# A fused SwiGLU feed-forward kernel: gate and up slices regrouped from 1, 2, 3, 3, 3 to 1, 1, 2, 4, 4 f chunks, two fillers ahead of the first projection dropped

## Chip, cores and metric

The kernel runs on one core of one Trainium2 chip. The metric is the device time of one execution in microseconds (us). A profiled execution also has a span, from the first to the last instruction, which is about 1.3 us shorter than its device time (162.8 against 164.1 for the profiled run of before).

## Reference

```python
B, S, D, F = 1, 2048, 640, 1536          # bf16
def reference(x, w_gate, w_up, w_down):
    g = silu(x @ w_gate)
    u = x @ w_up
    return (g * u) @ w_down
```

## The kernel before

F is cut into 12 chunks of 128 columns, S into four blocks of 512 rows. For each block and each f chunk, five matmuls make the gate projection `pg` and five the up projection `pu`; ScalarE and VectorE make `aT` from them; then `aT` is multiplied by the down weights. Weights stay resident after one load, in column slices of which each becomes usable only when all of it has landed. The first block is the special one: x comes in rows and is transposed by the tensor engine, and everything waits for first loads. The cut below is shortened, also between the lines that it shows.

```python
W_CHUNKS = [(0, 1), (1, 3), (3, 6), (6, 9), (9, 12)]   # f chunks per slice
N_WARM, N_GAP = 18, 2
...
load_x(nc.sync, 0, 1); load_x(nc.scalar, 2, 3)          # four chunks of 128 rows of x
load_x(nc.sync, 1, 2); load_x(nc.scalar, 3, 4)
for dst, src in ((wg_sb, wg_v), (wu_sb, wu_v)):         # slice 0 on both queues
    for eng, (k0, k1) in zip(queues, halves):
        eng.dma_start(out=dst[:, k0:k1, wslice(0, 1)], in_=src[:, k0:k1, wslice(0, 1)])
load_w(nc.sync, wg_sb, wg_v, *W_CHUNKS[1])              # slice 1: gate, then up
load_w(nc.sync, wu_sb, wu_v, *W_CHUNKS[1])
for a, b in W_CHUNKS[2:]:
    load_w(nc.sync, wg_sb, wg_v, a, b); load_w(nc.sync, wu_sb, wu_v, a, b)
nc.sync.dma_start(out=wd_sb[:], in_=wd_v)
... # cut
def warm(n):                                            # fillers: results unused
    for _ in range(n):
        nc.tensor.matmul(pw[:, 0:P], lhsT=ones[:], rhs=ones[:], start=True, stop=True)
... # cut; the head of the tensor engine, first block and first f chunk:
warm(N_WARM)
transpose_chunk(0, [(dve, "po_a", 0, KD)])
transpose_chunk(2, [(dve, "po_b", 0, KD)])
warm(N_GAP)
for c in (1, 3):
    transpose_chunk(c, [(act, "po_a", 0, 2), (dve, "po_b", 2, KD)])
warm(2)
proj_pair(pg, wg_sb, fc, sb, 0)                         # 5 matmuls, x chunks 0 and 2
proj_pair(pg, wg_sb, fc, sb, 1)                         # 5 matmuls, x chunks 1 and 3
proj(pu, wu_sb, fc, sb, 0, S_BLK)
```

## Time and profile before

| | before |
|---|---|
| time, first three runs | 163.87 us median (163.78 to 164.17) |
| span of the profiled run | 162.8 us |
| tensor engine busy | 98% |
| first projection starts | 5.30 us |
| second f chunk starts | 7.49 us |

A line of the timeline has the start in us, the duration in us, the engine, the line of the kernel, the operation, output and inputs, and how many were merged; brackets tell the idle time before it and what ended that. How fast the tensor engine ran is read from merged lines: ten 128-column matmuls at half rate start 107 ns apart and take about 1.27 us in all, at full rate 56 ns apart and 0.72 to 0.76 us; a gap between them makes a line longer. The tensor engine goes from half to full rate; this text calls that moment the release of the clock. The prediction shows the line of the second ten transposes (0.76 us, full rate). The first ten, from the tensor engine's timeline of the kernel before:

```profile
2.28 1.27 PE L189 MATMUL pt<-ident,x_sb 128*128 128x128 bf16 x10
3.35 0.42 PE L180 MATMUL pw<-ones 128*128 128x128 bf16 x2
```

1.27 us for ten is half rate, and so is 0.42 us for two. So in this one execution the clock was released between 3.35 and 4.23 us.

### The profile page before, as it was taken

Reading aid. Unit: us, or ns where it says so; the run is one execution under the profiler, and the core shown is the slowest. Engines: PE = TensorE matmul, PEld = TensorE weight load, DVE = VectorE, ACT = ScalarE, POOL = GpSimd, SP = SyncE. Lnnn points to the kernel's source line nnn. Section 1 sums busy time; section 2 is a strip of 40 time slices with the busy share of each in tenths; the row PEclk is TensorE's granted clock in tenths of the full one; section 3 lists DMA queues with packets and bytes.
Section 4 is the critical chain, followed back from the end, with each engine's and each line's share of the span. In section 5 each row is a group of like instructions: output and inputs, shape, how many; then the busy total and the mean of one; then the engine's idle time right before and its main releaser. Section 6 shows DMA issues by size and latency. Waiting matters only on the chain.

```text
span 162.8 us, 2081 instructions
## 1 busy us (share of the span) xinstructions
PE 159.7 (98%) x779; PEld 75.4 (46%) x779; DVE 111.8 (69%) x251; ACT 42.6 (26%) x73; POOL 0.6 (0%) x6
## 2 busy tenths in 40 slices
PE   8999999999999999999999999999999999999994
PEld 7644444444444444444444444444444444445442
DVE  2223333499559999979919999979964999993000
ACT  3322222212232222221222322221214222222121
POOL 1000000000000000000000000000000000000000
DMA  7999999993269993003110000000420000000312
GB/s 212 295 327 330 364 216 253 245 185 60 66 152 180 220 220 68 4 0 34 64 64 0 0 4 2 0 0 0 64 68 32 0 0 0 0 0 4 53 35 73
DMA packets 42585, 15.86 MB, mean 97 GB/s; under 512 B 33232, under 2 KB 42448, under 8 KB 42576
## 3 DMA queue, kind: packets, MB, share of 16 engines
q1 hardware_dynamic: 33664, 14.75, 37.2%
q10 hardware_dynamic: 8912, 0.98, 4.0%
q8 instruction: 6, 0.10, 0.3%
q14 instruction: 3, 0.02, 0.1%
HBM read 7.21 MB, written 2.62 MB: 60 GB/s over the span
## 4 chain that ended last, share of the span: by engine, by line
PE 95%; DMA 3%; SPq 0%; DVE 0%; issue 0%
PE pu L198 32%; PE pg L198 31%; PE po_a L281 25%; PE po_t L256 6%; DMA wg_sb<-in_w_gate_dram 3%; PE pg L213 1%; SPq L84 0%; PE po_b L298 0%; DVE ot_b L306 0%
## 5 line engine op out<-in xcount | busy, mean ns | idle before, releaser
L198 PE MATMUL pu<-xT,wu_sb 128*128 128x512 bf16 (+1 forms) x240 | 59.5, 379 | 0.0
L198 PE MATMUL pg<-xT,wg_sb 128*128 128x512 bf16 (+1 forms) x235 | 58.3, 379 | 0.0
L246 DVE TENSOR_TENSOR aT<-sg,pu 128x512 bf16<-128x512 f32 (+1 forms) x48 | 32.8, 683 | 32.0 <-PE pu L198 32.0
L245 ACT ACTIVATE sg<-pg 128x512 f32<-128x512 f32 (+1 forms) x48 | 28.6, 596 | 70.2 <-PE pg L198 65.7
L281 PE MATMUL po_a<-wd_sb,aT 128*128 128x512 bf16 x192 | 42.1, 379 | 0.0
L151 DVE SCALAR_TENSOR_TENSOR prod<-wgT,x_row 128x640 f32<-128x640 bf16 x48 | 39.4, 821 | 1.1
L151 DVE SCALAR_TENSOR_TENSOR prod<-wuT,x_row 128x640 f32<-128x640 bf16 x48 | 39.4, 821 | 1.0
L198 PEld LDWEIGHTS <-wu_sb 128*128 128x128 bf16 x240 | 23.5, 98 | 28.0
L198 PEld LDWEIGHTS <-wg_sb 128*128 128x128 bf16 x235 | 23.0, 98 | 27.6
L281 PEld LDWEIGHTS <-aT 128*128 128x128 bf16 x192 | 18.8, 98 | 22.5
L289 ACT CAST ot<-po_a 128x512 bf16<-128x512 f32 x16 | 9.4, 586 | 32.3 <-PE po_a L281 21.3
L256 PE MATMUL po_t<-aT,wd_sb 128*128 128x512 bf16 (+1 forms) x48 | 10.4, 366 | 0.0
L256 PEld LDWEIGHTS <-wd_sb 128*128 128x128 bf16 x48 | 4.7, 98 | 5.1
L306 DVE CAST ot_b<-po_b 128x128 bf16<-128x128 f32 x1 | 0.3, 291 | 9.9 <-PE po_b L298 9.9
L265 ACT CAST ot_t<-po_t 128x512 bf16<-128x512 f32 (+1 forms) x4 | 2.2, 560 | 11.6 <-PE po_t L256 11.6
L194 DVE COPY xT<-pt 128x640 bf16<-128x640 bf16 (+1 forms) x4 | 1.6, 425 | 3.4 <-PE pt L189 3.4
L151 DVE DVE_READ_ACCUMULATOR prod<-wuT,x_row 128x1 f32 x48 | 3.9, 82 | 0.0
L151 DVE DVE_READ_ACCUMULATOR prod<-wgT,x_row 128x1 f32 x48 | 3.9, 82 | 0.0
L267 DVE STREAM_TRANSPOSE ot_q<-ot_t 128x512 bf16<-128x512 bf16 (+1 forms) x4 | 2.7, 678 | 1.7 <-ACT ot_t L265 1.7
L180 PE MATMUL pw<-ones 128*128 128x128 bf16 x22 | 2.8, 304 | 0.4 <-DVE ones L104 0.4
L189 PE MATMUL pt<-ident,x_sb 128*128 128x128 bf16 x20 | 2.0, 268 | 0.5 <-DMA x_sb<-in_x_dram 0.5
L180 PEld LDWEIGHTS <-ones 128*128 128x128 bf16 x22 | 2.2, 143 | 0.4 <-DVE ones L104 0.4
(17 smaller groups left out, 9.0 us busy)
## 6 DMA issues: line engine op xcount, KB each, us to landing
out_dram<-ot SPq DMA_DIRECT2D x16, 128.0 KB, 1.7
wd_sb<-in_w_down_dram SPq DMA_DIRECT2D x1, 1920.0 KB, 12.6
wg_sb<-in_w_gate_dram SPq DMA_DIRECT2D x3, 480.0 KB, 7.1
wu_sb<-in_w_up_dram SPq DMA_DIRECT2D x3, 480.0 KB, 7.6
x_row<-in_x_dram SPq DMA_DIRECT2D x1, 640.0 KB, 4.8
out_dram<-ot_q ACTq DMA_DIRECT2D x12, 32.0 KB, 1.9
x_sb<-in_x_dram SPq DMA_DIRECT2D x2, 160.0 KB, 3.0
x_sb<-in_x_dram ACTq DMA_DIRECT2D x2, 160.0 KB, 3.2
```

Source lines behind the costliest of these rows:

```text
L151: nc.vector.scalar_tensor_tensor(out=prod[:], in0=wT[:, fc, :], scalar=1.0, in1=x_row[:, t, :], op0=ALU.mult, op1=ALU.mult, accum_out=acc[ ...
L180: nc.tensor.matmul(pw[:, 0:P], lhsT=ones[:], rhs=ones[:], start=True, stop=True)
L189: nc.tensor.transpose(out=pt[:, kd - k0, :], in_=x_sb[:, c, kd * P : (kd + 1) * P], identity=ident[:],)
L198: nc.tensor.matmul(ps[:, c0:c1], lhsT=w_sb[:, kd, fc * P : (fc + 1) * P], rhs=xT[:, kd, sb * S_BLK + c0 : sb * S_BLK + c1], start=(kd == 0 ...
L213: nc.tensor.matmul(pair(ps[:]), lhsT=w_sb[:, kd, fc * P : (fc + 1) * P], rhs=pair(xT[:, kd, sb * S_BLK : (sb + 1) * S_BLK]), start=(kd == ...
L245: nc.scalar.activation(sg[:, 0:n_s], pg[:, 0:n_s], ACT.Silu)
L246: nc.vector.tensor_tensor(out=aT[:, fc, s_sl], in0=sg[:, 0:n_s], in1=pu[:, 0:n_s], op=ALU.mult)
L256: nc.tensor.matmul(po_t[:], lhsT=wd_sb[:, kf, DA:D], rhs=aT[:, kf, sb * S_BLK : sb * S_BLK + n_t], start=(kf == 0), stop=(kf == KF - 1),)
L265: nc.scalar.copy(ot_t[:], po_t[:])
L267: nc.vector.transpose(out=ot_q[:], in_=ot_t[:])
L281: nc.tensor.matmul(po_a[:], lhsT=aT[:, kf, s0 : s0 + P], rhs=wd_sb[:, kf, 0:DA], start=(kf == 0), stop=(kf == KF - 1),)
L289: nc.scalar.copy(ot[:], po_a[:])
```

## The change

The intent is to have the second gate and up slices sooner (half the bytes), to make up for it with larger slices where there is slack, and to let the first projection start as soon as its slice is there.

```diff
-    W_CHUNKS = [(0, 1), (1, 3), (3, 6), (6, 9), (9, 12)]
+    W_CHUNKS = [(0, 1), (1, 2), (2, 4), (4, 8), (8, 12)]
@@ head of the tensor engine
                 for c in (1, 3):
                     transpose_chunk(c, [(act, "po_a", 0, 2), (dve, "po_b", 2, KD)])
-                warm(2)
                 proj_pair(pg, wg_sb, fc, sb, 0)
```

## The prediction

> **What bounds the kernel now.** I read the page first, then the waits of the tensor engine, then the timeline of the first 36 us, then the DMA issues and packet counts in short windows of the head. From the page, the header, the busy line and the chain of work that ended last:
>
> ```profile
> span 162.8 us, 2081 instructions
> ...
> PE 159.7 (98%) x779; PEld 75.4 (46%) x779; DVE 111.8 (69%) x251; ACT 42.6 (26%) x73; POOL 0.6 (0%) x6
> ...
> PE 95%; DMA 3%; SPq 0%; DVE 0%; issue 0%
> PE pu L198 32%; PE pg L198 31%; PE po_a L281 25%; PE po_t L256 6%; DMA wg_sb<-in_w_gate_dram 3%; PE pg L213 1%; SPq L84 0%; PE po_b L298 0%; DVE ot_b L306 0%
> ```
>
> The chain is tensor-engine work from end to end, except for one DMA: the load of the first gate slice, 3% of the span. Who made the tensor engine wait, over the whole span:
>
> ```profile
> PE pt L189 <- DMA x_sb<-in_x_dram: 0.5, 1, 0.5
> PE pw L180 <- DVE ones L104: 0.4, 1, 0.4
> PE pg L213 <- DMA wg_sb<-in_w_gate_dram: 0.2, 1, 0.2
> ```
>
> Three waits, 1.1 us in all, all in the first 5.3 us. There is no wait for a second or later weight slice, and none after the first projection started. So the kernel is a head of about 5.3 us followed by an unbroken stream of matmuls. A change to weight slices or fillers can gain only in the head, and can lose only if it opens a gap in the stream. The timeline of the head and of the first f chunks:
>
> ```profile
> 0.39 2.10 PE L180 MATMUL pw<-ones 128*128 128x128 bf16 x18 [0.39 <-DVE ones L104]
> ...
> 0.91 0.43 SPq L118 DMA_DIRECT2D wg_sb<-in_w_gate_dram  x1
> ...
> 2.18 0.37 SPq L81 DMA_DIRECT2D wg_sb<-in_w_gate_dram  x1
> ...
> 2.64 0.47 SPq L81 DMA_DIRECT2D wu_sb<-in_w_up_dram  x1
> ...
> 4.23 0.76 PE L189 MATMUL pt<-ident,x_sb 128*128 128x128 bf16 x10 [0.46 <-DMA x_sb<-in_x_dram]
> ...
> 4.83 0.28 PE L180 MATMUL pw<-ones 128*128 128x128 bf16 x2
> ...
> 5.30 1.27 PE L213 MATMUL pg<-xT,wg_sb 128*128 128x256 bf16 x10 [0.20 <-DMA wg_sb<-in_w_gate_dram]
> ...
> 7.27 0.96 PEld L198 LDWEIGHTS <-wg_sb 128*128 128x128 bf16 x5
> ...
> 8.35 0.96 PEld L198 LDWEIGHTS <-wu_sb 128*128 128x128 bf16 x5
> ```
>
> Two things are to be seen. First, the two fillers that the change drops start at 4.83 and are over at 5.11, and the first projection still waits 0.20 us after them, for the gate slice whose first half was issued at 0.91. Second, the second gate and up slices, issued at 2.18 and 2.64, are first read by the weight loads at 7.27 and 8.35. When they landed comes from the DMA issues of the window from 2.1 to 2.9 us (KB each, then us from issue to landing):
>
> ```profile
> wg_sb<-in_w_gate_dram SPq DMA_DIRECT2D x1, 320.0 KB, 4.6
> wu_sb<-in_w_up_dram SPq DMA_DIRECT2D x1, 320.0 KB, 5.3
> ```
>
> That is 2.18 + 4.6 = 6.8 and 2.64 + 5.3 = 7.9 us: 0.5 and 0.4 us ahead of need. These are the tightest deadlines among the later weight slices. The third slices, read the same way in the window from 4.1 to 4.8, landed at 4.20 + 5.2 = 9.4 and 4.61 + 6.3 = 10.9 against first uses at 11.59 and 12.67.
>
> **What the Trainium skill says.** "DMA: Bandwidth & Descriptors", section Specifications, gives 512 B as the smallest transfer for line rate. A one-chunk slice has rows of 128 bf16, 256 B, so the change puts two more loads below it. The trace agrees that packet size sets the rate. Packet counts in three windows, 4.3 to 5.0 us (about half 256 B), 5.0 to 7.0 (nearly all 512 B), and 8 to 14 (nearly all 768 B):
>
> ```profile
> DMA packets 468, 0.17 MB, mean 244 GB/s; under 512 B 245, under 2 KB 468, under 8 KB 468
> ...
> DMA packets 1146, 0.59 MB, mean 297 GB/s; under 512 B 28, under 2 KB 1146, under 8 KB 1146
> ...
> DMA packets 2619, 1.96 MB, mean 327 GB/s; under 512 B 64, under 2 KB 2619, under 8 KB 2619
> ```
>
> The same page, section Queues, rings and completion order, says that on each DMA engine descriptors are consumed in ring order, and that the engine alternates between the queues it has work for at packet granularity. So a second slice on the Sync queue stands behind the Sync part of the first slices on each engine and cannot make it land sooner; only the halves on the Scalar queue share with it. The view of DMA issues agrees for order: on the Sync queue the slices land in the order issued.
>
> "TensorE: Matmul & The Clock Gate", Part 1, says that the array starts at half rate, that about 3.4 us of sustained activity releases it, and that about an idle window of the same length throttles it again; a 128-column matmul starts every 107 ns cold and every 56 ns warm. The trace agrees with the spacing: 18 fillers take 2.10 us, (2.10 - 0.31) / 17 = 105 ns apart (0.31 being one cold matmul's length); the ten transposes at 4.23 take 0.76 us including a gap between their two groups. So the rate is full before the two dropped fillers run.
>
> **The change part by part.**
>
> 1. *Two fillers removed.* Two 128-column matmuls and their two weight loads go: the instruction order shows 1556 tensor-engine rows instead of 1560, and no engine's other work changes place. They occupy the array for 2 x 56 = 112 ns, and end before the gate slice lands. Without them the engine is free about 0.11 us sooner and waits 0.31 instead of 0.20 us for the same slice. On the path: 0.00 us. If the slice lands sooner in some execution, at most 0.11 us is gained.
>
> 2. *First gate slice.* Its size, queues and issue do not change, and what follows it on the Sync queue stands behind it. Start of the first projection stays at 5.3 us, with some tenths of jitter as for any first landing.
>
> 3. *Second slices, 160 KB each instead of 320 KB.* The 256 B rate I estimate from the first window above: 223 packets of 512 B are 114 KB, which at 297 GB/s take 0.38 of the 0.70 us; the 245 packets of 256 B, 63 KB, then took 0.32 us, about 200 GB/s. A one-chunk slice of 164 thousand bytes takes 0.82 us, against 328 thousand / 297 = 1.10 us for the two-chunk slice. The gate slice then lands near 6.8 - 0.3 = 6.5 (needed 7.27) and the up slice near 7.3 (needed 8.35). The slack goes from 0.5 and 0.4 to about 0.8 and 1.0 us. No tensor-engine wait existed there, so nothing is saved.
>
> 4. *Later slices.* Chunks 2 and 3 come next, 1.10 us each: about 8.4 and 9.5, needed at 9.43 and 10.51 (the starts of those weight loads in the timeline): slack 1.0. Then the four-chunk slices, 655 thousand bytes; 1024 B packets should run at least as fast as the 327 GB/s of the 768 B ones, so 2.0 us each: about 11.5 and 13.5, needed at 13.75 and 14.83: slack 2.2 and 1.3. The last pair lands near 15.5 and 17.5, needed at 22.38 and 23.46. Every deadline is met, and the smallest slack grows from 0.4 to about 0.8 us.
>
> 5. *What follows.* The same bytes pass through the queue in about the same time (the last up slice landed at 9.19 + 8.9 = 18.1 before), so the down weights and the turned inputs come no later. The down weights were issued at 10.66 with 12.6 to landing, 23.3, and are needed at 31.0.
>
> Sum on the path: 0.0 (fillers) + 0.0 (slices) = 0.0 us, with up to 0.1 us of gain in an execution where the first gate slice comes early.
>
> **The rivals.**
>
> *A: the four-chunk slices come too late and open a gap.* For it: a slice must land whole before its first chunk may be used, and a four-chunk one carries 33% more than a three-chunk one. Against it: slack 1.3 us at its tightest by step 4; the queue's rate in the 4.3 to 14 us stretch would have to fall by more than 10% to eat it. It would cost some tenths of a us: 164.0 to 164.5.
>
> *B: the small packets of the second slices slow the first slices on the Scalar queue or the DMA as a whole.* For it: 256 B packets move at about 200 instead of 297 GB/s. Against it: there are half as many bytes, and a shorter packet lets the other queue's turn come sooner. It could shift the first projection by 0.1 to 0.2 us either way.
>
> *C: without the fillers the clock drops or rises late.* For it: the fillers are there to keep the tensor engine active. Against it: full rate is seen at 4.23, and the idle time grows by 0.11 us only. If in some execution the release came a whole 3.4 us window later, half rate for that window loses 1.7 us, 165.5 us or 1.0%, still inside 2%.
>
> *D: in unprofiled executions the second slice does come late in the kernel before, and the smaller slice removes a wait that the profile did not catch.* The slack of 0.4 us leaves room for it; it would gain 0.1 to 0.3 us: 163.5 to 163.7. The three timed runs differ by only 0.39 us, so no larger wait can hide in some of them.
>
> **Range and chances.** The centre is the time before, 163.87, less a few hundredths for rival D and early landings: 163.8. The range is the spread of the three runs (163.78 to 164.17) widened down by the largest of D's gain and up by a little jitter: 163.45 to 164.2. 2% is 3.3 us; the head waits for DMA or fillers 1.1 us in all, so a gain of 3.3 us is out of reach, and a loss of 3.3 us is twice rival C at its worst. Chances: faster 0.01, same 0.98, slower 0.01.
>
> **What would show it right or wrong.** Right: in the changed kernel's waits the first projection waits for the gate slice about 0.3 us instead of 0.2 and starts within 0.2 us of 5.30; the tensor engine has no other wait after it; the second slices land near 6.5 and 7.3; the gap from the start of the first projection to the end of the span is unchanged within 0.1 us. Wrong: a tensor-engine wait for the weights at the third, fifth or ninth f chunk (rival A), a first projection that starts over 0.2 us sooner or later (B), the first projections at half rate (C), or a time below 163.45 without any of these.

## More of the kernel before

All runs told here are in the fast state, with a granted clock of 1.000 in the records (0.999 in one execution of run 6). That clock is not the half and full rate of the tensor engine that this text speaks of: the rate is read from how far apart matmuls start.

## The result and the profile after

| | before | changed |
|---|---|---|
| median of six runs | 163.91 us (163.53 to 164.17) | 164.34 us (163.81 to 164.45) |
| span of the profiled run | 162.8 us | 163.0 us |
| first projection starts | 5.30 us | 5.09 us |
| second f chunk starts | 7.49 us | 7.65 us |

The ratio of changed to before is 1.0018, 95% interval 0.9997 to 1.0039. A ratio here is the mean time of one kernel's fast runs over the mean of the other's fast runs of the same rounds, so it is not quite the ratio of the medians. The median lies 0.14 us above the range that was stated.

The chain of the changed kernel, by engine and by line, from its page:

```profile
PE 97%; DMA 2%; DVE 0%; issue 0%
PE pu L198 32%; PE pg L198 31%; PE po_a L280 25%; PE po_t L255 6%; DMA x_sb<-in_x_dram 2%; PE pt L189 1%; PE pg L213 1%; PE po_b L297 0%; DVE ot_b L305 0%; PE pw L180 0%
```

The DMA in the chain is now that of x, not of the gate slice. All waits of its tensor engine (us in total, times, longest):

```profile
PE pw L180 <- DVE ones L104: 0.4, 1, 0.4
PE pt L189 <- DMA x_sb<-in_x_dram: 0.3, 1, 0.3
```

The wait for the gate slice is gone altogether, and there is none for a later slice. The tensor engine's timeline in the head:

```profile
2.77 1.25 PE L189 MATMUL pt<-ident,x_sb 128*128 128x128 bf16 x10 [0.28 <-DMA x_sb<-in_x_dram]
3.81 0.42 PE L180 MATMUL pw<-ones 128*128 128x128 bf16 x2
4.03 1.27 PE L189 MATMUL pt<-ident,x_sb 128*128 128x128 bf16 x10
5.09 1.64 PE L213 MATMUL pg<-xT,wg_sb 128*128 128x256 bf16 x10
6.57 1.24 PE L198 MATMUL pu<-xT,wu_sb 128*128 128x512 bf16 x5
```

Three things differ from before. The first transposes start at 2.77 instead of 2.28, because x landed later, although no load of x was changed. The second transposes take 1.27 instead of 0.76 us: still half rate. And the first projection starts 0.21 us sooner but takes 1.64 us instead of 1.27, because the clock is released in the middle of it. After that the two traces are alike: from the start of the second f chunk to the end of the span there are 162.8 - 7.49 = 155.3 us before and 163.0 - 7.65 = 155.3 us after. So the whole difference of these two executions is made in the first 7.7 us, by the time of the first landings and by the moment of the release.

The slices did what was worked out. Issues in the windows from 2.7 to 3.3, 3.7 to 5.3 and 5.7 to 6.3 us of the changed kernel (KB each, us from issue to landing):

```profile
wg_sb<-in_w_gate_dram SPq DMA_DIRECT2D x1, 160.0 KB, 3.6
wu_sb<-in_w_up_dram SPq DMA_DIRECT2D x1, 160.0 KB, 3.8
...
wg_sb<-in_w_gate_dram SPq DMA_DIRECT2D x1, 320.0 KB, 4.6
wu_sb<-in_w_up_dram SPq DMA_DIRECT2D x1, 320.0 KB, 5.1
...
wg_sb<-in_w_gate_dram SPq DMA_DIRECT2D x1, 640.0 KB, 6.2
wu_sb<-in_w_up_dram SPq DMA_DIRECT2D x1, 640.0 KB, 7.5
```

They were issued at 2.75, 3.16, 3.73, 4.31, 5.22 and 5.79 us, so they landed at 6.4, 7.0, 8.3, 9.4, 11.4 and 13.3, against 6.5, 7.3, 8.4, 9.5, 11.5 and 13.5 worked out.

### The profile page after: what moved, and what is told of

Read it like the earlier page. It is cut to its first block, busy times and chain, and to the rows that moved or that the text cites. A ratio compares the mean times of both kernels' runs of the same rounds, so it can differ in the third digit from the quotient of the medians.

```text
span 163.0 us, 2077 instructions
## 1 busy us (share of the span) xinstructions
PE 160.2 (98%) x777; PEld 76.0 (47%) x777; DVE 111.9 (69%) x251; ACT 42.7 (26%) x73; POOL 0.6 (0%) x6
## 4 chain that ended last, share of the span: by engine, by line
PE 97%; DMA 2%; DVE 0%; issue 0%
PE pu L198 32%; PE pg L198 31%; PE po_a L280 25%; PE po_t L255 6%; DMA x_sb<-in_x_dram 2%; PE pt L189 1%; PE pg L213 1%; PE po_b L297 0%; DVE ot_b L305 0%; PE pw L180 0%
## 5 line engine op out<-in xcount | busy, mean ns | idle before, releaser
L189 PE MATMUL pt<-ident,x_sb 128*128 128x128 bf16 x20 | 2.5, 313 | 0.3 <-DMA x_sb<-in_x_dram 0.3
L189 PEld LDWEIGHTS <-x_sb 128*128 128x128 bf16 x20 | 2.1, 146 | 0.5 <-DMA x_sb<-in_x_dram 0.5
```

Of the source, the lines that this page charges most:

```text
L189: nc.tensor.transpose(out=pt[:, kd - k0, :], in_=x_sb[:, c, kd * P : (kd + 1) * P], identity=ident[:],)
```

## Experiments

Three theories stood against each other. P: the difference is not the change's; each execution draws its own time of release and its own first landings, and six of one kernel drew worse than six of the other. F: the dropped fillers make it slower, for instance by delaying the release. S: the slices make it slower. All runs gave results equal to the reference within its tolerance.

### 1 and 2: both kernels again, unchanged

No edit.

> The kernel before, unchanged, as a control for noise. Theory P (the time of a single execution is set by when the tensor clock is released in the head, a phase that no kernel chooses): its ratio to itself is within 0.3% of 1, single runs spread over 163.5 to 164.5 us, and the profile has the first projection (ten 256-column matmuls) at 1.27 us if the release came ahead of it and up to 2.3 us if not. Theories F (the dropped fillers) and S (the slices) expect 163.9 with a spread of 0.4 us and a projection at 1.27 us.

> The changed kernel, unchanged. P: same distribution as the control, median 163.7 to 164.3, ratio within 0.2% of 1, some executions early and some late in the release. F and S: again 164.3, ratio 1.002 to 1.004.

Measured: the kernel before 164.09 us (163.88 to 164.41), ratio to the other runs of itself 1.001 (0.9993 to 1.0027). The changed kernel 163.68 us (163.58 to 164.19), ratio 0.9988 (0.9968 to 1.0007). The order of the two is now reversed. The tensor engine's timeline of the control, from the last fillers on:

```profile
4.79 0.42 PE L180 MATMUL pw<-ones 128*128 128x128 bf16 x2
5.01 1.48 PE L213 MATMUL pg<-xT,wg_sb 128*128 128x256 bf16 x10
6.33 1.24 PE L198 MATMUL pu<-xT,wu_sb 128*128 128x512 bf16 x5
```

and that of the changed kernel's second profile:

```profile
3.35 0.38 PE L180 MATMUL pw<-ones 128*128 128x128 bf16 x2
3.56 0.90 PE L189 MATMUL pt<-ident,x_sb 128*128 128x128 bf16 x10
4.91 1.26 PE L213 MATMUL pg<-xT,wg_sb 128*128 128x256 bf16 x10 [0.44 <-DMA wg_sb<-in_w_gate_dram]
6.01 1.24 PE L198 MATMUL pu<-xT,wu_sb 128*128 128x512 bf16 x5
```

The roles have changed over. Now it is the kernel before whose fillers run at half rate (0.42 us for two) and whose first projection is slowed, 1.48 us; and it is the changed kernel that is released early (its two fillers take 0.38 us, between the 0.42 of half and the 0.28 of full rate, so the release comes at their end; the 0.90 us of the ten transposes is full rate with gaps among them, the longest 0.19 us from start to start) and waits 0.44 us for its gate slice, as step 1 of the prediction had it. P holds in its main point; F and S, which expected 164.3 again for the changed kernel, do not.

### 3 and 4: each half of the change alone

```diff
 e3: -    W_CHUNKS = [(0, 1), (1, 3), (3, 6), (6, 9), (9, 12)]
     +    W_CHUNKS = [(0, 1), (1, 2), (2, 4), (4, 8), (8, 12)]
 e4: -                warm(2)        # the one ahead of the first projection
```

> The new slices with the two fillers kept. S: 164.3 us, ratio 1.002 to 1.004, with the first gate slice landing or a later weight wait to show for it. F: 163.9, ratio 1.000. P: ratio within 0.2% of 1 either way.

> The old slices with the two fillers dropped. F: 164.3 us, ratio 1.002 to 1.004, with the first projection at half rate for part of its length in most executions. S: 163.9, ratio 1.000. P: ratio within 0.2% of 1.

Measured: slices alone 163.88 us (163.42 to 164.69), ratio 1.0002 (0.9977 to 1.0026); fillers alone 163.96 (163.62 to 164.37), ratio 1.0002 (0.9984 to 1.0021). Neither part makes 164.3 as F and S asked. The profiled execution of the fillers-only kernel did have a late release, as F expected of most (from projection to second chunk 2.54 us in the table below, against 2.18 in that of slices only), but so had one of the kernel before in run 1. The single executions of one kernel spread over as much as 1.27 us in these sets. Each interval reaches about 0.2% to either side of 1, so that a part's own effect of some 0.3 us is not excluded by its run alone. Taken together with the other sets, four of the changed kernel and all those of before (below), no half stands out.

### 5 and 6: the head pinned

If the spread is made in the head, a head in which neither the release nor a landing decides must take it away.

```diff
-    N_WARM, N_GAP = 18, 2
+    N_WARM, N_GAP = 110, 2
     nc.vector.memset(ones[:], 1.0)
+    pad = consts.tile([P, D], bf16)
+    nc.vector.memset(pad[:], 1.0)
+    for _ in range(11):                       # dummy work ahead of the xT copies
+        nc.vector.scalar_tensor_tensor(out=prod[:], in0=pad[:], scalar=1.0,
+            in1=pad[:], op0=ALU.mult, op1=ALU.mult)
```

> The kernel before with a pinned head: 110 fillers ahead of the transposes, so that the clock is released before the first projection whatever its phase, and eleven dummy vector operations ahead of the xT copies, so that the projection starts at a time that neither the clock nor a landing decides (about 11.5 us). P: span about 11.5 + 157.5 = 169.0 us, time near 170, and the spread of single executions falls from about 0.9 us to 0.2 or less. F and S say nothing of the spread; if the spread comes from anything after the head it stays at 0.8 us or more.

> The changed kernel with the same pinned head. P: the same time as the pinned kernel before within 0.1 us, and the same narrow spread. S by a later weight wait: slower than it by 0.3 us or more.

Measured, four runs each: pinned before 171.43 us (171.25 to 171.53), pinned changed 171.29 us (171.23 to 171.34). The absolute time was guessed 1.4 us too low (the projection starts as expected at 11.5 us, but the stretch from it to the end is about 1 us longer than in the other kernels. The last group of matmuls, `po_b`, starts 152.4 us after the second f chunk in both, 159.89 - 7.49 us before and 166.20 - 13.76 us here, so the microsecond comes after it; why is not known). What the runs were for came out: the spread fell to 0.28 and 0.11 us, the first a little over the 0.2 expected. On the same chip, eleven runs of the kernel before spread over 0.94 us (163.75 to 164.69); four drawn from those eleven have a spread of 0.28 or less in about 6% of draws and of 0.11 or less in under 1%. The pinned head takes away both draws, release and landings, and does not tell them apart. The timelines, pinned before and then pinned changed:

```profile
0.40 7.63 PE L186 MATMUL pw<-ones 128*128 128x128 bf16 x110 [0.40 <-DVE ones L104]
...
11.31 0.33 PE L195 MATMUL pt<-ident,x_sb 128*128 128x128 bf16 x3 [1.77 <-DVE xT L200]
11.48 0.27 PE L186 MATMUL pw<-ones 128*128 128x128 bf16 x2
11.59 1.26 PE L219 MATMUL pg<-xT,wg_sb 128*128 128x256 bf16 x10
```

```profile
0.40 8.50 PE L186 MATMUL pw<-ones 128*128 128x128 bf16 x110 [0.40 <-DVE ones L104]
...
11.31 0.33 PE L195 MATMUL pt<-ident,x_sb 128*128 128x128 bf16 x3 [0.90 <-DVE xT L200]
11.47 1.25 PE L219 MATMUL pg<-xT,wg_sb 128*128 128x256 bf16 x10
```

The same 110 fillers take 7.63 us in one and 8.50 in the other: each matmul that runs at half instead of full rate costs 107 - 56 = 51 ns, so the release came about 17 matmuls, or 17 x 107 ns = 1.8 us, later in the second. That difference ends in a wait of 1.77 against 0.90 us and no longer reaches the projection. The last transposes start at 11.31 us in both. And here the two fillers show by themselves: with nothing left to wait for, the projection starts at 11.59 with them and at 11.47 without, 0.12 us. That is also about the difference of the medians, 0.14 us, though the four times of each overlap and would not show it alone.

### 7: no fillers at the start

```diff
-    N_WARM, N_GAP = 18, 2
+    N_WARM, N_GAP = 0, 2
```

> The kernel before without the 18 fillers at the start: tensor work then begins with the transposes at about 2.3 us. P[...]: release between 5.5 and 9 us, the projections at half rate until then, median 0.4 to 1.2 us slower (164.4 to 165.2) and a wider spread, 1.5 us. If the release does not hang on activity: median unchanged at 164.0.

Measured: 164.37 us (164.04 to 165.52), ratio 1.0027 (0.9997 to 1.0057), the spread 1.48 us. The profiled execution took 165.06 us:

```profile
5.11 2.34 PE L213 MATMUL pg<-xT,wg_sb 128*128 128x256 bf16 x10
7.25 1.37 PE L198 MATMUL pu<-xT,wu_sb 128*128 128x512 bf16 x5
```

All ten matmuls of the projection run at half rate (2.34 us), and the first of the next group. That a tensor engine which begins later is released later fits this, but is not shown: in run 8 the release came later still, with fillers from 0.39 us on. The median is just below what was expected (164.4 to 165.2), and the interval still holds 1, so the direction is not settled either.

### 8 and 11: the changed kernel a third and a fourth time

No edit.

> The changed kernel a third time. P: median anywhere from 163.6 to 164.4, and the ratio over all three sets within 0.1% of 1. F and S: 164.3.

> The changed kernel a fourth time, for the pooled comparison: so far 18 executions with a mean of 164.07 against 45 of the kernel before with 164.03. P: median between 163.6 and 164.4, the mean over all four sets within 0.25 us of the kernel before. If the first set (164.34) was the true one: above 164.25.

Measured: 164.10 us (163.50 to 165.91), ratio 0.9988 (0.9961 to 1.0015); and 163.77 (163.42 to 164.27), ratio 0.9977 (0.9941 to 1.0012). The ratio 0.9988 cannot have the 165.91 us in it: all six over all eleven give 1.0009. The profiled execution of the third set was that slowest one, 165.91 us:

```profile
4.77 1.25 PE L189 MATMUL pt<-ident,x_sb 128*128 128x128 bf16 x10 [1.00 <-DMA x_sb<-in_x_dram]
5.81 2.34 PE L213 MATMUL pg<-xT,wg_sb 128*128 128x256 bf16 x10
```

Here both draws are bad: x came at 4.77, and the whole projection ran at half rate. That is the late release of rival C at its worst. The kernel before also has a time of this size, 165.59 us, among the runs taken beside the fourth set; that one was not profiled, so its cause is not known.

Pooled over all its sets, the changed kernel has 24 executions with a mean of 164.00 us, and the kernel before 56 with 164.06: a difference of -0.06 us with a standard error of 0.12.

### 9: ten more fillers

```diff
-                warm(2)
+                warm(12)
```

> The kernel before with twelve fillers ahead of the first projection instead of two, ten more. What fillers cost where they stand on the path: released, 10 x 56 ns less a wait of up to 0.4 us that they fill; not released, 10 x 107 ns, of which half is won back because the projection starts later and at a higher rate. I expect 0.2 to 0.6 us more, 164.2 to 164.6, so two fillers are worth 0.1 us at most. If fillers cost nothing: 164.0. If they are what releases the clock in time (theory F): no slower, or faster, than 163.9.

Measured: 164.86 us (163.96 to 165.12), ratio 1.0042 (1.0015 to 1.0069), so 0.69 us more in the mean (0.0042 x 164), a little over the 0.2 to 0.6 expected. Its profile is of the fastest of the six, 163.96 us, and does not show the cost. Theory F, by which fillers ahead of the projection help, is wrong here: they cost about 0.07 us each. By that, two are worth about 0.14 us, which agrees with the 0.12 us of the pinned pair and is lost in a spread of a microsecond.

### 10: a slice that does come too late

```diff
-    W_CHUNKS = [(0, 1), (1, 2), (2, 4), (4, 8), (8, 12)]
+    W_CHUNKS = [(0, 1), (1, 2), (2, 8), (8, 12)]
```

> The changed kernel with slices of one, one, six and four chunks, so that a slice does come too late: six chunks are 983 thousand bytes, 2.9 us at 340 GB/s, behind second slices that landed at 7.0. Gate lands at 9.9 (needed at 9.5), up at 12.8 (needed at 10.6): tensor waits of 0.4 and about 1.8 us at the third f chunk, 166.2 us, ratio 1.013. If the slices' deadlines are not as worked out from rates: no wait, 164.0.

Measured: 167.00 us (165.77 to 167.48), ratio 1.0173 (1.0138 to 1.0207); slower, while the verdict at 2% is "unclear". Its tensor engine's longest waits, and then the issues of the two large slices:

```profile
PE pu L198 <- DMA wu_sb<-in_w_up_dram: 1.4, 1, 1.4
PE pg L198 <- DMA wg_sb<-in_w_gate_dram: 1.2, 1, 1.2
```

```profile
wg_sb<-in_w_gate_dram SPq DMA_DIRECT2D x1, 960.0 KB, 6.4
wu_sb<-in_w_up_dram SPq DMA_DIRECT2D x1, 960.0 KB, 8.7
```

The way of working out deadlines holds: late slices show as tensor waits at the third f chunk, 2.6 us in all against 2.2 expected, and the time follows (3.15 us between the medians). The error begins with the first: issued at 4.37, the gate slice landed at 10.8 and not 9.9. The queue moved only 0.24 MB (235 GB/s) from 6 to 7 us, before it reached 377 to 385 GB/s: the second slices were through before the large one's packets came. The up slice, next in the queue, landed at 13.5 and not 12.8. A reader who works out landings from rates should also ask how long after its issue a transfer's packets begin. This also shows that rival A is a real way to lose, 1.7%, with no more than a bad choice of slices; the changed kernel's slices are simply not there.

### 12: hardly any idle time in the head

```diff
-    N_WARM, N_GAP = 18, 2
+    N_WARM, N_GAP = 21, 7         # on the changed kernel
```

> The changed kernel with 21 fillers at the start and 7 in the gap between the two pairs of transposes, in place of 18 and 2, so that the tensor engine hardly idles before the projection. If idle gaps delay the release of the clock: release always before about 4.5 us, median 163.6 to 163.8 and a narrower spread than 0.6 us. If the release comes at a phase that the gaps do not touch: median 164.1 to 164.5 (up to eight more fillers of 107 or 56 ns, part of them in place of waits), spread unchanged.

Measured: 164.13 us (163.53 to 164.59), ratio 0.9993 (0.9957 to 1.0029). The spread is 1.06 us, no narrower than others. Its one profile, of the fastest of the six, has an early release; the other five, up to 164.59, give no sign that filling the gaps makes it early in each execution. This is not a better version; a small effect of gaps is not excluded.

### All profiles side by side

From each timeline: when the first projection starts, how long it is from there to the second f chunk (2.18 us at full rate throughout), when that chunk starts, the span, and the rest, as differences of the rounded times. Runs 5, 6 and 10 are left out, as their head or their waits differ.

| profiled run | projection starts | to second chunk | second chunk starts | span | rest |
|---|---|---|---|---|---|
| before | 5.30 | 2.19 | 7.49 | 162.8 | 155.3 |
| changed | 5.09 | 2.56 | 7.65 | 163.0 | 155.3 |
| 1, before again | 5.01 | 2.40 | 7.41 | 162.7 | 155.3 |
| 2, changed again | 4.91 | 2.18 | 7.09 | 162.4 | 155.3 |
| 3, slices only | 4.84 | 2.18 | 7.02 | 162.3 | 155.3 |
| 4, fillers only | 5.22 | 2.54 | 7.76 | 163.1 | 155.3 |
| 7, no early fillers | 5.11 | 3.34 | 8.45 | 163.7 | 155.3 |
| 8, changed, third | 5.81 | 3.48 | 9.29 | 164.6 | 155.3 |
| 9, twelve fillers | 5.19 | 2.17 | 7.36 | 162.6 | 155.2 |
| 11, changed, fourth | 4.62 | 2.18 | 6.80 | 162.1 | 155.3 |
| 12, dense head | 4.71 | 2.18 | 6.89 | 162.2 | 155.3 |

The last column is the same in all: without rounding, 155.28 to 155.31. What varies is the start, over 1.2 us, and the rate of the first two groups, over 1.3 us. Both vary among executions of the same kernel.

## Why the prediction was wrong

What it said of the change's own cost held; the step that failed is rival C, the time of the release, which it set aside, and with it the path of the head and the range. Of the changed kernel's four medians three lie inside the stated range (163.68, 164.10, 163.77) and the first, 164.34, does not, so the miss is also a matter of luck. Point by point:

- *Step 1, fillers.* Right as to their cost, with one omission. The traces count four tensor-engine rows fewer, as it said. They cost nothing while a wait for the gate slice follows (run 2: a wait of 0.44 us where before had 0.20) and 0.11 us at most at full rate where none does; the pinned pair showed 0.12. Where the release is late they cost 0.21 us (run 1: 4.79 to 5.01), which the step did not count; part of that comes back in the projection, which then begins later and runs less of its length at half rate.
- *Step 2, the start of the first projection.* Its path held only in part, and its size was wrong. That the projection ends a wait for the gate slice is seen in three of six profiles of the two kernels (before, run 2, and run 11, where the weight load waited 0.3 us); in the changed kernel's first profile and in runs 1 and 8 the transposes or the fillers after them, at half rate, were last, and the expected wait of 0.3 us was not there. "5.3 us, with some tenths of jitter" was 4.62 to 5.81 us in four profiles of the very same changed kernel (4.62, 4.91, 5.09, 5.81).
- *Steps 3 to 5, slices.* Right, to 0.1 to 0.3 us for most and 0.5 us at worst (the last up slice landed at 17.0 in place of 17.5). The estimate of 200 GB/s for 256 B packets was too low: run 10's 699 packets from 4.2 to 4.9 us, all under 512 B, moved at 246 GB/s, and six such windows of that run and the changed kernel at 224 to 281. It did not matter, because the slack was never used.
- *Rival A*: not seen. *Rival B*: it cannot be told from the spread. Its sign, a first projection over 0.2 us off, was met (5.09, and 4.62 to 5.81 over the four), but the gate slice's Sync half landed at 4.67 to 5.26 us in five profiles with the old slices (before, runs 1, 4, 7, 9) and at 4.57 to 5.70 in seven with one-chunk second slices, and a shift of 0.1 to 0.2 us would be lost in that. *Rival D*: a wait for the second slice was seen in no profile of the kernel before, nor in runs 4, 7 and 9, which have its slices.
- *Rival C*: this is the step that failed. It was set aside with "full rate is seen at 4.23", one execution's release taken for that of all. Its sign, "the first projections at half rate", is what the changed kernel's first profile shows for part of the projection, 1.64 us in place of 1.27. In the changed kernel's own four profiles the release came ahead of the projection in two, within it in one and after it in one; in the kernel before, ahead of it in one and within it in the other. It is not special to the change, as rival C had it, but a term of the times of either kernel, worth up to 1.3 us between the projection's start and the second chunk (2.18 to 3.48 us); the prediction reckoned 1.7 us for it and left it out of the range.
- *The range.* "The spread of the three runs" was 0.39 us. That of 56 runs of the same kernel is 163.53 to 165.59. Drawing six of these 56 at random many times, the middle 80% of medians is 163.83 to 164.17, and about 1% are 164.34 or more. A range for the median of six should have had some 0.2 us to each side of 164.0 from this alone; even so the first set was a rare draw.

P explains the difference as chance, and three facts carry this: the changed kernel's three further sets of six gave 163.68, 164.10 and 163.77; the pooled difference is -0.06 us with an error of 0.12; and pinning the head takes most of the spread away. What stays open: why the first set was so high (whether executions that follow each other, or of one chip, draw alike was not tested; with the 24 times dealt at random into four sets, the sets' ranks lie as far apart as here in about 7% of deals, so the record does not settle it), and whether a true gain of about 0.1 us is there, which the pinned pair suggests and the unpinned runs are too few to show.

"TensorE: Matmul & The Clock Gate", Part 1, of the Trainium skill says that the activity window is free-running and that the same kernel has different numbers of slow matmuls from run to run. The traces agree in that respect: the same 110 fillers took 7.63 and 8.50 us. That the window's phase is the cause was not shown; no run here can set it.

## What to carry to other kernels

Before a range is stated for a change of tenths of a percent, find out what one execution draws by chance: several profiles of the *same* kernel show it, where one profile makes the draw look like a property of the kernel. Subtract a fixed tail from the span (here 155.3 us) and the noise stands alone in the head. And a load that lands ahead of its first use gives nothing by landing sooner; ask for the wait before cutting the slice.

## What the Trainium skill lacked or had wrong

- "TensorE: Matmul & The Clock Gate", Part 1: it puts the transition around 4 us into sustained matmul activity, ±500 ns from run to run. Here it varied more. In the pinned pair, whose 110 fillers follow each other without a gap, the 7.63 and 8.50 us mean that about 26 and 43 of them ran at half rate, so the release came about 2.8 and 4.6 us after the first matmul. In the changed kernel, with gaps, it came before the ten transposes that start at 3.56 us (run 2), while in run 8 the projection from 5.81 us on was at half rate through all its 2.34 us (after a wait of 1.00 us ahead of the transposes). This makes part of the range of 163.42 to 165.91 us of one kernel. The page's other remark, that the cold count varies from run to run, agrees.
- "DMA: Bandwidth & Descriptors", Specifications: its row that gives 512 B as the smallest transfer for line rate is too coarse if taken by itself. The rate rose on above 512 B: 224 to 281 GB/s at 256 B (six windows of run 10 and the changed kernel), 297 at 512 B and 327 at 768 B (before), 348 at 1024 B (changed, 8.5 to 15 us), 377 to 385 at 1536 B (run 10, 7 to 10.5 us). These windows differ in more than packet size, so this is no clean measurement of it.
- No page has how much first landings vary: the second Sync chunk of x, issued at 0.45 us, took 2.7 us to land in one execution of the changed kernel (run 2) and 4.3 us in another (run 8).
